# Two row tiles of a state-space stage moved ahead in a fused state-space and MLP kernel

## The chip, the cores and the metric

The kernel runs on one NeuronCore of a Trainium2 chip. The metric is the device time of one execution in microseconds (us); less is better. Five engines work side by side, each in the order of its own instruction stream: TensorE (PE), VectorE (DVE), ScalarE (ACT), GpSimd (POOL) and SyncE (SP), which here issues nearly all loads and stores. PSUM, into which PE writes, has eight banks of 512 float32 columns.

## The reference, cut to what matters

The input x has 2048 rows of 640. Two branches are computed and mixed, row by row, by a gate:

```python
g = sigmoid((x * gate_w).sum(-1, keepdims=True))
# branch a: a diagonal complex state-space layer
Lam_bar = exp(dt * Lam);  Bu = x @ B_bar.T          # P = 640 complex states
h[t] = Lam_bar * h[t-1] + Bu[t]                     # t = 0 .. 2047
a = 2 * real(hseq @ Cmat.T) + x * Dskip
# branch b: an MLP
b = gelu(x @ w1 + b1) @ w2 + b2                     # 640 -> 1728 -> 640
return g * a + (1 - g) * b
```

## The kernel before, in words

Time is cut into four chunks of 512 rows (CH). A chunk passes through four stages.

`ssm(c)` is the state stage. For each of five row tiles of 128 states (ks), PE multiplies x by the real and the imaginary part of B (BT_re, BT_im; five matmuls of 512 columns each), ACT copies both results out of PSUM to bf16 (`bu`, L602), and VectorE runs `scan_ops`: three products (f1 to f3) with tables of cosines and sines (TCOS, TSIN), which turn the complex recurrence into two real ones, two scans with the factor r_c (f4, L548), and three products back (f6 to f8) into `hs`. ACT turns the scan's end for the next chunk (`carry`, four small instructions, L556).

`ff1(c)` is the first MLP layer: thirteen tiles of 128 hidden columns (kf = 0 to 12), each of five matmuls of 512 columns (L300), and a gelu on ACT into `gel` (L309). W1 lies in three strips, w1a (tiles 0 to 5), w1b (6 to 9) and w1c (10 to 13). The last tile (`last_tile`, L324) is computed the other way round, on a bank that ACT first fills with its bias (`last_bank`, L317). Its last column is the gate: gate_w is copied into w1c as one more column (L441, POOL). ACT writes the tile's gelu to `gelN` and SP turns it with two transposing DMAs (L332).

`fin_b(c)` is the second MLP layer as a Strassen product: seven half-size products (L697) from sums of blocks of gel and W2. Three weight sums, TA, TB and TC, are built once, while chunk 1's `ff1` runs: ACT writes the negated W2 blocks to TA and TB (`w_minus`, L647), POOL adds the others with accumulating DMAs (`w_plus`, L642). `fin_a(c)` multiplies the states by C (L775), and VectorE mixes both branches with the gate columns `gcol` (L613 to L615, from `gates`), L780. `fold(ks)` multiplies the factor (Lam_bar - 1) / Lam into C, ACT first (L504, L506) and VectorE then (L510); it needs nothing of the scan. The last chunk's C product is a Strassen product too (`fin_s`, L837).

The order of work is written out by hand and is the program order of each engine. VectorE's order is set by a planner: `Clock` holds estimated times of PE, ACT and DVE; `later` queues a VectorE step with a due time and a cost, `let_out` issues those that by their estimated start come before a given time, `dve_now` first lets out what is due and then issues its own step. `small` holds the carries for ACT until PE's clock has passed their due time (`settle`). The estimates change only the order, not the work.

SP's order around the change: w1a strips 4 and 3 (L132), w1b (L164), w1c (L166), b1x (L182), four transposing loads of B (L184, L185: BT_re and BT_im of row tiles 0 and 1, then of 2 to 4), the transposing load of x's second chunk (L186), and, behind chunk 0's last tile, the gelN transposes (L332), W2 (`load_w2`, L197 to L206) and C (L209, L210).

Of the kernel before, what the change touches and what calls it, by code (L numbers as in the profile page):

```python
# [10 lines left out]
ALU = mybir.AluOpType  # L11
# [31 lines left out]
def kernel(  # L43
# [32 lines left out]
    def bank(dtype=F32):  # L76
        return ps.tile([P, CH * 4 // (4 if dtype == F32 else 2)], dtype, name="bank")
# [53 lines left out]
    def load_w1a(queue, kd):  # L131
        queue.dma_start(out=w1a[kd], in_=B_w1[kd * P:(kd + 1) * P, 0:cut1])  # L132
# [27 lines left out]
    load_turned(H)  # L160
    load_w1a(nc.sync, 4)
    load_w1a(nc.sync, 3)
    for kd in range(KD):
        nc.sync.dma_start(out=w1b[kd], in_=B_w1[kd * P:(kd + 1) * P, cut1:cut2])  # L164
    for t, k0, k1 in ((w1c_lo, 0, 3), (w1c_hi, 3, KD)):
# [14 lines left out]
    for i, m in enumerate((1.0, float(CH), float(CH // 2), float(2 * HC - 2))):  # L180
        nc.gpsimd.memset(tf[:, i:i + 1], m)
    nc.sync.dma_start(out=b1x[:, 0:F_LAST], in_=B_b1[F - F_LAST:F].rearrange("(o d) -> o d", o=1).to_broadcast([P, F_LAST]))  # L182
    for r0, r1, part in ((0, KSA * P, 0), (KSA * P, KS * P, 1)):
        nc.sync.dma_start_transpose(out=BT_re[part][:], in_=A_B_re[r0:r1, :])  # L184
        nc.sync.dma_start_transpose(out=BT_im[part][:], in_=A_B_im[r0:r1, :])  # L185
    nc.sync.dma_start_transpose(out=xT[1][:], in_=x2d[CH:2 * CH, :])  # L186
    nc.gpsimd.memset(gelN[:, :, F_LAST:P], 0.0)
    for k in range(2):
# [19 lines left out]
    def load_CT():  # L208
        nc.sync.dma_start_transpose(out=CT_re[:], in_=A_C_re[:, :])  # L209
        nc.sync.dma_start_transpose(out=CT_im[:], in_=A_C_im[:, :])  # L210
# [7 lines left out]


    class Clock:  # L220
        pe = 3.4
        act = 12.0
        dve = 0.0

# [204 lines left out]
        ff1_mm(banks[kf], 0, kf, 3, 0, CH, False, 3)  # L429
    for kf in range(FA):  # L430
        ff1_act(banks[kf], 0, kf)
    two_banks = [bank(), bank()]
    for kd in range(KD):
        for i in range(2):
            ff1_mm(two_banks[i], 0, FA + i, kd)
    for i in range(2):
        ff1_act(two_banks[i], 0, FA + i)
    nc.scalar.activation(out=thr[:], in_=dtl[:], func=ACT.Tanh, scale=0.5)
    act(0.2)
    for t, k0, k1 in ((w1c_lo, 0, 3), (w1c_hi, 3, KD)):  # L440
        nc.gpsimd.tensor_copy(out=t[:, :, n1c - 1:n1c], in_=colB[:, k0:k1].rearrange("p (k o) -> p k o", o=1))  # L441
    ff1(0, FA + 2)
    load_w2()
    load_CT()

    for dst, r in ((sq, 0), (cq, 1)):
        nc.vector.tensor_copy(out=dst[:].rearrange("p (n k) -> p k n", n=NQ), in_=FSC[:, r * KS:(r + 1) * KS, 0:NQ])
# [9 lines left out]

    nsL = col("nsL")
    nc.gpsimd.tensor_scalar(out=nsL[:], in0=sL, scalar1=-1.0, scalar2=None, op0=ALU.mult)
    nc.gpsimd.tensor_scalar(out=inv[:, KS:2 * KS], in0=thr[:], scalar1=-1.0, scalar2=1.0, op0=ALU.mult, op1=ALU.add)  # L460
    nc.gpsimd.tensor_scalar(out=thr[:], in0=thr[:], scalar1=1.0, scalar2=None, op0=ALU.add)
    around(TCOS, cM, sM, ALU.subtract, ALU.add)
    around(TSIN, sM, cM, ALU.add, ALU.subtract)
    nc.vector.tensor_copy(out=TCOS[:, :, HB:HB + HC], in_=FC)
# [6 lines left out]
    nc.vector.tensor_scalar(out=TSIN[:, :, HB - 1:0:-1], in0=TSIN[:, :, HB + 1:CH], scalar1=-1.0, scalar2=None, op0=ALU.mult)  # L471
    nc.vector.tensor_copy(out=TSIN2[:, :, 0, CH - 1:0:-1], in_=TSIN[:, :, 1:CH])
    nc.vector.reciprocal(out=inv[:], in_=inv[:])
    ck.dve = 20.0


    c2re = col("c2re"); n2re = col("n2re"); n2im = col("n2im")

    def factors():
        tt = lambda o, a, b, op: nc.gpsimd.tensor_tensor(out=o, in0=a, in1=b, op=op)  # L480
        a_c = col("a_c"); b_c = col("b_c")
        den = inv[:, 0:KS]
        tt(r_c[:], thr[:], inv[:, KS:2 * KS], ALU.mult)
        tt(a_c[:], r_c[:], cth, ALU.mult)
        tt(b_c[:], r_c[:], sth, ALU.mult)
        nc.gpsimd.tensor_scalar(out=a_c[:], in0=a_c[:], scalar1=-1.0, scalar2=None, op0=ALU.add)
        nc.gpsimd.tensor_scalar(out=den, in0=den, scalar1=2.0, scalar2=None, op0=ALU.mult)
        tt(q1[:], a_c[:], lre_c, ALU.mult)
        tt(q2[:], b_c[:], lim_c, ALU.mult)
        tt(q1[:], q1[:], q2[:], ALU.add)  # L490
        tt(c2re[:], q1[:], den, ALU.mult)
        tt(q1[:], a_c[:], lim_c, ALU.mult)
        tt(q2[:], b_c[:], lre_c, ALU.mult)
        tt(q1[:], q1[:], q2[:], ALU.subtract)
        tt(n2im[:], q1[:], den, ALU.mult)
        nc.gpsimd.tensor_scalar(out=n2re[:], in0=c2re[:], scalar1=-1.0, scalar2=None, op0=ALU.mult)
# [26 lines left out]
    def scan_ops(c, ks, bu, ready):  # L523
        wide = lambda t: t[:, ks:ks + 1, :].to_broadcast([P, 2, CH])
        sines = TSIN2[:, ks, :, :]
        s = {}

        def tt(o, a, b, op):
            nc.vector.tensor_tensor(out=o, in0=a, in1=b, op=op)  # L529

        def f1():
            s["mc"] = work.tile([P, 2, CH], BF16, name="wa", bufs=1)
            tt(s["mc"][:], wide(TCOS), bu[:], ALU.mult)

        def f2():
            s["ms"] = work.tile([P, 2, CH], BF16, name="wb", bufs=1)
            tt(s["ms"][:], sines, bu[:], ALU.mult)

        def f3():
            s["v"] = work.tile([P, 2, CH], BF16, name="v", bufs=1)  # L540
            tt(s["v"][:], s["mc"][:], s["ms"][:, ::-1, :], ALU.add)

        def f4(ri):
            if ri == 0:
                settle(1)
                s["g"] = work.tile([P, 2, CH], BF16, name="g")
            init = 0.0 if c == 0 else carry[:, ri, ks:ks + 1]
            nc.vector.tensor_tensor_scan(s["g"][:, ri, :], r_c[:, ks:ks + 1].to_broadcast([P, CH]),  # L548
                                         s["v"][:, ri, :], init, ALU.mult, ALU.add)

        def f5():
            g = s["g"]

            def turn_carry():
                m = work.tile([P, 2], F32, name="e1")
                one = lambda out, i, sc, b: nc.scalar.activation(out=out, in_=g[:, i, CH - 1:CH], func=ACT.Identity,  # L556
                                                                 scale=sc[:, ks:ks + 1], bias=b)
                one(m[:, 0:1], 1, nsL, 0.0)
                one(m[:, 1:2], 0, sL, 0.0)
                one(carry[:, 0, ks:ks + 1], 0, cL, m[:, 0:1])  # L560
                one(carry[:, 1, ks:ks + 1], 1, cL, m[:, 1:2])
                ck.act += 0.6

            small.append((ck.dve + 2.0, turn_carry))

        def f6():
            s["no"] = work.tile([P, 2, CH], BF16, name="wa", bufs=1)
            tt(s["no"][:], wide(TCOS), s["g"][:], ALU.mult)

        def f7():  # L570
            s["ns"] = work.tile([P, 2, CH], BF16, name="wb", bufs=1)
            tt(s["ns"][:], sines, s["g"][:], ALU.mult)

        def f8():
            to = lambda t: t.rearrange("p r (i t) -> p r i t", i=2)
            dst = hs[c][:].rearrange("p i r k t -> p r i k t")[:, :, :, ks, :]
            tt(dst, to(s["no"][:]), to(s["ns"][:, ::-1, :]), ALU.subtract)

        later(ready, 0.68, f1)
        later(0, 0.62, f2)  # L580
        later(0, 0.65, f3)
        later(0, 1.27, lambda: f4(0))
        later(0, 1.21, lambda: f4(1))
        if c < NCH - 1:
            later(0, 0.0, f5)
        later(0, 0.69, f6)
        later(0, 0.62, f7)
        later(0, 0.64, f8, c)

    def ssm(c, at={}):  # L590
        hs[c] = hsp.tile([P, 2, 2, KS, HT], BF16, name="hs")
        for ks in range(KS):
            if ks in at:
                at[ks]()
            bu = work.tile([P, 2, CH], BF16, name="bu", bufs=8)
            for ri, BT in enumerate((BT_re, BT_im)):
                p = bank()
                for kd in range(KD):
                    nc.tensor.matmul(p[:], lhsT=BT[ks >= KSA][:, kd, (ks % KSA if ks < KSA else ks - KSA) * P:][:, 0:P], rhs=xT[c][:, kd, :],  # L599
                                     start=(kd == 0), stop=(kd == KD - 1))  # L600
                    pe(CH)
                nc.scalar.activation(out=bu[:, ri, :], in_=p[:], func=ACT.Identity)  # L602
                act(0.6)
            scan_ops(c, ks, bu, ck.act)
            let_out(ck.pe)
            settle()


    def gates(c):
        sl = slice(c * TPC, (c + 1) * TPC)  # L610

        def f():
            nc.vector.tensor_scalar(out=gcol[:, 0, sl], in0=gz[:, sl], scalar1=0.5, scalar2=0.5, op0=ALU.mult, op1=ALU.add)  # L613
            nc.vector.tensor_scalar(out=gcol[:, 1, sl], in0=gz[:, sl], scalar1=-0.5, scalar2=0.5, op0=ALU.mult, op1=ALU.add)
            nc.vector.tensor_scalar(out=gcol[:, 2, sl], in0=gz[:, sl], scalar1=0.5, scalar2=-0.5, op0=ALU.mult, op1=ALU.add)  # L615

        dve_now(ck.pe, 0.2, f)


    HALVES = ((0, HD), (HD, D))  # L620
# [280 lines left out]
    def sums(c):  # L901
        return {0: lambda: minus_c(c), 1: lambda: minus_d(c)}

    ssm(0)
    gel_tile(1)

    ff1(1, 0, {3: lambda: (w_minus(0), w_plus(TA, B12)),
               5: lambda: (w_minus(1), w_plus(B12, TB)),
               9: lambda: (first_sums(), w_plus(TB, TA), w_plus(TC, TB))})
    gates(0)  # L910
    ssm(1, {3: lambda: fold(0)})
# [63 lines left out]
```

## Time and profile before

| | |
|---|---|
| median of three runs | 208.58 us (208.19 to 208.94) |
| the profiled execution | 208.8 us, of which the profile's span is 207.0 us |
| granted PE clock | 1.00 |
| PE busy | 201.8 us (98%) |
| VectorE busy | 180.5 us (87%) |
| ACT busy | 143.9 us (69%) |
| chunk 0: `ff1`, then `ssm` on PE | first w1a matmul 3.96, w1b 11.44, w1c 16.03, last tile 19.27, `ssm` 19.88 us |
| chunk 1: `ff1`, last tile, `ssm` on PE | 30.67, 45.37, 45.97 us |
| first state product on VectorE | 22.87 us |

Times on the profile's axis count from the start of the span. A row of the list of waits names the instruction that waited, then what released it, then the total, the count and the longest. A row of the chain has start, length and what it was; "x20" counts merged instructions. SPq is the sequencer of SP, which issues DMAs; its rows in a timeline last as long as the issue, and the data lands later. PEld is PE's weight load, which runs ahead of the matmuls.

### The profile page before, as it was taken

The numbers are of one execution on the slowest core, as the hardware profiler recorded it, in microseconds if no ns is written. First come the engines' busy times: TensorE is split into PE (matmuls) and PEld (weight loads), VectorE is DVE, ScalarE is ACT, GpSimd is POOL, SyncE is SP. The second block draws the span as 40 slices with busy tenths as digits, with TensorE's granted clock in tenths as the row PEclk, the third lists the DMA queues.
The fourth block names the chain that finished last, engine by engine and source line by source line (L and its number), as shares of the span: only waits on it lengthen the run. The fifth ranks groups of instructions, "written<-read, shape, count | busy, mean of one in ns | idle before, by whom it ended". The sixth has DMA issues, their size and how long they took to land.

```text
span 207.0 us, 3588 instructions
## 1 busy us (share of the span) xinstructions
PE 201.8 (98%) x1311; PEld 120.3 (58%) x1311; DVE 180.5 (87%) x282; ACT 143.9 (69%) x291; POOL 45.6 (22%) x81
## 2 busy tenths in 40 slices
PE   8999999999999999999999999999999999999993
PEld 5745444444467644675457777544447777777762
DVE  2694599999499999699999999999999999998673
ACT  4699656999888799992666893358986595067720
POOL 8426100313410410031001061200420136016000
PEclk9999999999999999999999999999999999999999
DMA  6999989999899070269913279920675729949703
GB/s 190 233 206 213 177 220 298 176 212 218 152 181 220 16 117 6 69 115 245 205 42 66 59 139 216 258 85 0 79 158 105 161 79 194 194 130 164 124 2 127
DMA packets 45126, 30.28 MB, mean 146 GB/s; under 512 B 26834, under 2 KB 42548, under 8 KB 45108
## 3 DMA queue, kind: packets, MB, share of 16 engines
q0 software_dynamic: 6448, 12.53, 35.3%
q1 hardware_dynamic: 38084, 17.03, 34.6%
q10 hardware_dynamic: 576, 0.49, 0.8%
q8 instruction: 10, 0.16, 0.3%
q14 instruction: 8, 0.07, 0.1%
HBM read 7.79 MB, written 2.62 MB: 50 GB/s over the span
## 4 chain that ended last, share of the span: by engine, by line
PE 76%; SPq 14%; ACT 4%; DMA 3%; issue 1%; DVE 0%; DVEq 0%; ACTq 0%
PE bank L697 26%; PE bank L775 16%; PE bank L599 16%; PE bank L300 14%; PE bank L837 4%; DMA w_sb<-in_B_w_dram 3%; SPq L184 2%; SPq L185 2%; SPq L186 2%; ACT gel L309 2%; SPq L197 1%; SPq L157 1%; SPq L332 1%; SPq L164 1%; PE bank L324 1%
## 5 line engine op out<-in xcount | busy, mean ns | idle before, releaser
L548 DVE TENSOR_TENSOR_SCAN g<-r_c,carry,v 128x512 bf16<-128x512 f32 x30 | 37.5, 1274 | 0.9
L602 ACT ACTIVATE bu<-bank 128x512 bf16<-128x512 f32 x40 | 23.5, 596 | 21.0 <-PE bank L599 21.0
L309 ACT ACTIVATE gel<-bank,colB 128x512 bf16<-128x512 f32 (+1 forms) x52 | 33.0, 692 | 3.9 <-PE bank L300 3.5
L697 PEld LDWEIGHTS <-gel 128*128 128x128 bf16 x280 | 27.3, 98 | 11.1 <-issue 0.2
L775 PEld LDWEIGHTS <-hs 128*128 128x128 bf16 x240 | 23.4, 98 | 9.0
L697 PE MATMUL bank<-w_sb,gel 128*128 128x320 bf16 x168 | 24.3, 299 | 0.0
L300 PEld LDWEIGHTS <-w1a_sb 128*128 128x128 bf16 x162 | 13.9, 97 | 12.2 <-issue 0.3
L775 PE MATMUL bank<-CT_re,hs 128*128 128x320 bf16 x120 | 20.2, 299 | 0.0
L775 PE MATMUL bank<-CT_im,hs 128*128 128x320 bf16 x120 | 20.2, 299 | 0.0
L717 ACT ACTIVATE gb<-bank,gcol 128x320 f32<-128x320 f32 x32 | 15.8, 524 | 5.2 <-PE bank L697 5.2
L529 DVE TENSOR_TENSOR wa<-TCOS,bu 128x1024 bf16<-128x1024 bf16 x20 | 13.8, 690 | 5.8 <-ACT bu L602 5.1
L709 ACT ACTIVATE bank<-bank 128x320 f32<-128x320 f32 x16 | 6.8, 423 | 14.3 <-DVE ot L780 8.1
L599 PEld LDWEIGHTS <-BT_im 128*128 128x128 bf16 x100 | 9.8, 98 | 11.8
L599 PEld LDWEIGHTS <-BT_re 128*128 128x128 bf16 x100 | 9.6, 98 | 11.0
L529 DVE TENSOR_TENSOR hs<-wa,wb 128x1024 bf16<-128x1024 bf16 x20 | 13.8, 690 | 0.6
L529 DVE TENSOR_TENSOR v<-wa,wb 128x1024 bf16<-128x1024 bf16 x20 | 13.8, 690 | 0.6
L300 PE MATMUL bank<-xA,w1a_sb 128*128 128x128 bf16 (+2 forms) x102 | 14.1, 291 | 0.2 <-DVE xA L269 0.2
L529 DVE TENSOR_TENSOR wa<-TCOS,g 128x1024 bf16<-128x1024 bf16 x20 | 13.8, 689 | 0.4
L529 DVE TENSOR_TENSOR wb<-TSIN,g 128x1024 bf16<-128x1024 bf16 x20 | 13.7, 684 | 0.0
L529 DVE TENSOR_TENSOR wb<-TSIN,bu 128x1024 bf16<-128x1024 bf16 x20 | 13.7, 684 | 0.0
L300 PEld LDWEIGHTS <-w1b_sb 128*128 128x128 bf16 x80 | 7.8, 98 | 9.8 <-DMA w1b_sb<-in_B_w_dram 0.8
L697 PEld LDWEIGHTS <-N 128*128 128x128 bf16 x112 | 11.0, 98 | 4.3
(183 smaller groups left out, 370.2 us busy)
## 6 DMA issues: line engine op xcount, KB each, us to landing
out_dram<-ot SPq DMA_DIRECT2D x15, 160.0 KB, 4.6
w_sb<-in_B_w_dram SPq DMA_DIRECT2D x4, 480.0 KB, 6.5
gb<-gq POOLq DMA_DIRECT2D x6, 320.0 KB, 5.9
gel<-N POOLq DMA_DIRECT2D x4, 448.0 KB, 4.6
xn<-in_A_x_dram SPq DMA_DIRECT2D x10, 160.0 KB, 3.6
N<-gel POOLq DMA_DIRECT2D x3, 448.0 KB, 4.4
gel<-gel POOLq DMA_DIRECT2D x3, 448.0 KB, 6.8
N<-N POOLq DMA_DIRECT2D x3, 448.0 KB, 7.7
```

Of the source, the lines that this page charges most:

```text
L184: nc.sync.dma_start_transpose(out=BT_re[part][:], in_=A_B_re[r0:r1, :])
L300: nc.tensor.matmul(p[:, t0:t1], lhsT=w, rhs=xT[c][:, kd, t0:t1], start=(kd == 0) if first is None else first, stop=(kd == last), skip_grou ...
L309: nc.scalar.activation(out=dst, in_=src, func=ACT.Gelu_apprx_tanh, bias=b1_c[p0:p1, kf:kf + 1])
L529: nc.vector.tensor_tensor(out=o, in0=a, in1=b, op=op)
L548: nc.vector.tensor_tensor_scan(s["g"][:, ri, :], r_c[:, ks:ks + 1].to_broadcast([P, CH]), s["v"][:, ri, :], init, ALU.mult, ALU.add)
L599: nc.tensor.matmul(p[:], lhsT=BT[ks >= KSA][:, kd, (ks % KSA if ks < KSA else ks - KSA) * P:][:, 0:P], rhs=xT[c][:, kd, :], start=(kd == 0 ...
L602: nc.scalar.activation(out=bu[:, ri, :], in_=p[:], func=ACT.Identity)
L697: nc.tensor.matmul(p[:, 0:HD], lhsT=lhs[:, s, j * P:(j + 1) * P], rhs=rhs[:, s, :], start=fresh and s == 0, stop=s == KH - 1, skip_group_c ...
L709: nc.scalar.activation(out=quad[j][dst][:, 0:HD], in_=quad[j][src][:, 0:HD], func=ACT.Identity)
L717: nc.scalar.activation(out=gbs[ti][:, h * HD:(h + 1) * HD], in_=quad[j][name][:, 0:HD], func=ACT.Identity, scale=gcol[:, 1, ti:ti + 1])
L775: nc.tensor.matmul(p[:, 0:d1 - d0], lhsT=hs[c][:, a // H, j // KS, j % KS, (a % H) * P:][:, 0:P], rhs=CT[:, j % KS, d0:d1], start=False, s ...
L837: nc.tensor.matmul(t[j][:, d0:d1], lhsT=A[i][:, k, j * P:(j + 1) * P], rhs=B[i][:, k, d0:d1], start=fresh and k == 0, stop=k == KS - 1, sk ...
```

## The change

The transposing loads of BT_re and BT_im for row tiles 0 and 1 are issued by SP right behind w1a, ahead of w1b, w1c and b1x. The matmuls and evictions of row tiles 0 and 1 of chunk 0's state stage (`inputs(0, range(KSA))`) are issued right behind the six w1a tiles: first both BT_re groups, then both BT_im groups. The rest of chunk 0's `ff1`, `load_w2` and `load_CT` follow, and `ssm(0)` is left with row tiles 2 to 4.

On POOL, the two instructions that prepare `inv` and `thr` and the product r_c come ahead of the copy of the gate columns into w1c. In chunk 1's `ff1`, the two negations of W2 with their accumulating DMAs move from tiles 3 and 5 to tiles 5 and 7. The planner's PE clock starts at 5.9 instead of 3.4, VectorE's is 17.8 instead of 20.0 behind the tables, three of its costs are larger, and `gates` is due by ACT's clock in chunks 1 to 3. With these clocks the planner issues the folds and the gate columns later in VectorE's order.

```diff
     load_w1a(nc.sync, 4)
     load_w1a(nc.sync, 3)
+    def load_BT(part, r0, r1):
+        nc.sync.dma_start_transpose(out=BT_re[part][:], in_=A_B_re[r0:r1, :])
+        nc.sync.dma_start_transpose(out=BT_im[part][:], in_=A_B_im[r0:r1, :])
+    load_BT(0, 0, KSA * P)
     for kd in range(KD):
         nc.sync.dma_start(out=w1b[kd], in_=B_w1[kd * P:(kd + 1) * P, cut1:cut2])
...
-    for r0, r1, part in ((0, KSA * P, 0), (KSA * P, KS * P, 1)):
-        nc.sync.dma_start_transpose(out=BT_re[part][:], in_=A_B_re[r0:r1, :])
-        nc.sync.dma_start_transpose(out=BT_im[part][:], in_=A_B_im[r0:r1, :])
+    load_BT(1, KSA * P, KS * P)
...
-        pe = 3.4
+        pe = 5.9
...
     for kf in range(FA):
         ff1_act(banks[kf], 0, kf)
-    two_banks = [bank(), bank()]
-    ...
     nc.scalar.activation(out=thr[:], in_=dtl[:], func=ACT.Tanh, scale=0.5)
     act(0.2)
-    for t, k0, k1 in ((w1c_lo, 0, 3), (w1c_hi, 3, KD)):
-        nc.gpsimd.tensor_copy(out=t[:, :, n1c - 1:n1c], in_=colB[:, k0:k1]...)
-    ff1(0, FA + 2)
-    load_w2()
-    load_CT()
+    nc.gpsimd.tensor_scalar(out=inv[:, KS:2 * KS], in0=thr[:], ...)
+    nc.gpsimd.tensor_scalar(out=thr[:], in0=thr[:], ...)
...
     nc.vector.reciprocal(out=inv[:], in_=inv[:])
-    ck.dve = 20.0
+    nc.gpsimd.tensor_tensor(out=r_c[:], in0=thr[:], in1=inv[:, KS:2 * KS], op=ALU.mult)
+    for t, k0, k1 in ((w1c_lo, 0, 3), (w1c_hi, 3, KD)):
+        nc.gpsimd.tensor_copy(out=t[:, :, n1c - 1:n1c], in_=colB[:, k0:k1]...)
+    ck.dve = 17.8
+
+    def inputs(c, rows):
+        bus = [work.tile([P, 2, CH], BF16, name="bu", bufs=8) for _ in rows]
+        ready = []
+        for ri, BT in enumerate((BT_re, BT_im)):
+            for bu, ks in zip(bus, rows):
+                p = bank()
+                for kd in range(KD):
+                    nc.tensor.matmul(p[:], lhsT=BT[ks >= KSA][:, kd, ...][:, 0:P], rhs=xT[c][:, kd, :], ...)
+                    pe(CH)
+                nc.scalar.activation(out=bu[:, ri, :], in_=p[:], func=ACT.Identity)
+                ready.append(act(0.6))
+        return list(zip(bus, ready[-len(bus):]))
+
+    early = inputs(0, range(KSA))
+    two_banks = [bank(), bank()]
+    ...                                  # w1b tiles 6 and 7, as before
+    ff1(0, FA + 2)
+    load_w2()
+    load_CT()
...
-        later(0, 0.62, f2)
-        later(0, 0.65, f3)
+        later(0, 0.65, f2)
+        later(0, 0.75, f3)
...
-        later(0, 0.64, f8, c)
+        later(0, 0.7, f8, c)
...
-            scan_ops(c, ks, bu, ck.act)
+            scan_ops(c, ks, *(given[ks] if ks < len(given) else inputs(c, [ks])[0]))
...
-        dve_now(ck.pe, 0.2, f)                                       # in gates(c)
+        dve_now(ck.act + 0.3 if c > 0 else ck.pe, 0.2, f)
...
-    ssm(0)
+    ssm(0, {}, early)
     gel_tile(1)
-    ff1(1, 0, {3: lambda: (w_minus(0), w_plus(TA, B12)),
-               5: lambda: (w_minus(1), w_plus(B12, TB)),
+    ff1(1, 0, {5: lambda: (w_minus(0), w_plus(TA, B12)),
+               7: lambda: (w_minus(1), w_plus(B12, TB)),
                9: lambda: (first_sums(), w_plus(TB, TA), w_plus(TC, TB))})
```

More of the change, by code (lines that the diff above doesn't have):

```diff
@@ L431 @@
         ff1_act(banks[kf], 0, kf)
-    two_banks = [bank(), bank()]
[L433 to L437, printed above, removed]
     nc.scalar.activation(out=thr[:], in_=dtl[:], func=ACT.Tanh, scale=0.5)
     act(0.2)
-    for t, k0, k1 in ((w1c_lo, 0, 3), (w1c_hi, 3, KD)):
-        nc.gpsimd.tensor_copy(out=t[:, :, n1c - 1:n1c], in_=colB[:, k0:k1].rearrange("p (k o) -> p k o", o=1))
-    ff1(0, FA + 2)
-    load_w2()
-    load_CT()
+    nc.gpsimd.tensor_scalar(out=inv[:, KS:2 * KS], in0=thr[:], scalar1=-1.0, scalar2=1.0, op0=ALU.mult, op1=ALU.add)
+    nc.gpsimd.tensor_scalar(out=thr[:], in0=thr[:], scalar1=1.0, scalar2=None, op0=ALU.add)
     for dst, r in ((sq, 0), (cq, 1)):
@@ L459 @@
     nc.gpsimd.tensor_scalar(out=nsL[:], in0=sL, scalar1=-1.0, scalar2=None, op0=ALU.mult)
-    nc.gpsimd.tensor_scalar(out=inv[:, KS:2 * KS], in0=thr[:], scalar1=-1.0, scalar2=1.0, op0=ALU.mult, op1=ALU.add)
-    nc.gpsimd.tensor_scalar(out=thr[:], in0=thr[:], scalar1=1.0, scalar2=None, op0=ALU.add)
     around(TCOS, cM, sM, ALU.subtract, ALU.add)
@@ L473 @@
     nc.vector.reciprocal(out=inv[:], in_=inv[:])
-    ck.dve = 20.0
+    nc.gpsimd.tensor_tensor(out=r_c[:], in0=thr[:], in1=inv[:, KS:2 * KS], op=ALU.mult)
+    for t, k0, k1 in ((w1c_lo, 0, 3), (w1c_hi, 3, KD)):
+        nc.gpsimd.tensor_copy(out=t[:, :, n1c - 1:n1c], in_=colB[:, k0:k1].rearrange("p (k o) -> p k o", o=1))
+    ck.dve = 17.8
[6 more added lines that the diff above has]
+                for kd in range(KD):
+                    nc.tensor.matmul(p[:], lhsT=BT[ks >= KSA][:, kd, (ks % KSA if ks < KSA else ks - KSA) * P:][:, 0:P], rhs=xT[c][:, kd, :],
+                                     start=(kd == 0), stop=(kd == KD - 1))
+                    pe(CH)
[4 more added lines that the diff above has]
+    two_banks = [bank(), bank()]
+    for kd in range(KD):
+        for i in range(2):
+            ff1_mm(two_banks[i], 0, FA + i, kd)
+    for i in range(2):
+        ff1_act(two_banks[i], 0, FA + i)
+    ff1(0, FA + 2)
+    load_w2()
+    load_CT()
     c2re = col("c2re"); n2re = col("n2re"); n2im = col("n2im")
@@ L482, in factors @@
         den = inv[:, 0:KS]
-        tt(r_c[:], thr[:], inv[:, KS:2 * KS], ALU.mult)
         tt(a_c[:], r_c[:], cth, ALU.mult)
@@ L587, in scan_ops, with ssm @@
         later(0, 0.62, f7)
-        later(0, 0.64, f8, c)
-    def ssm(c, at={}):
+        later(0, 0.7, f8, c)
+    def ssm(c, at={}, given=()):
         hs[c] = hsp.tile([P, 2, 2, KS, HT], BF16, name="hs")
@@ L594, in ssm @@
                 at[ks]()
[L595 to L603, printed above, removed]
-            scan_ops(c, ks, bu, ck.act)
+            scan_ops(c, ks, *(given[ks] if ks < len(given) else inputs(c, [ks])[0]))
             let_out(ck.pe)
```

## The prediction

> **What bounds the kernel now.** I read the page's busy table first, then the list of who waited for whom, then the chain of work in order of time between 28 and 57 us, then the timelines of SP, ACT and DVE over the first 50 us.
>
> ```profile
> span 207.0 us, 3588 instructions
> PE 201.8 (98%) x1311; PEld 120.3 (58%) x1311; DVE 180.5 (87%) x282; ACT 143.9 (69%) x291; POOL 45.6 (22%) x81
> ```
>
> TensorE (PE) is the bound. Its rows run at an unchanging pace: a group of five 512-column matmuls starts every 1.08 us (L599 starts at 19.88, 20.96, 22.04), a whole state stage takes 10.79 us each time, a fin_b 13.31 us, a fin_a 10.87 us. The change adds and removes no matmul, so it can only move the places in which PE stands still. The list of waits has few of them:
>
> ```profile
> PEld L300 <- DMA w1b_sb<-in_B_w_dram: 0.8, 2, 0.6
> PE bank L324 <- ACT bank L317: 0.5, 1, 0.5
> DVE wa L529 <- ACT bu L602: 5.1, 1, 5.1
> DVE CT_re L510 <- issue: 3.1, 1, 3.1
> ```
>
> The first row is W1's second strip arriving late. Weight loads run ahead of matmuls, so the 0.8 us costs PE less: the 20 w1b matmuls of chunk 0 start at 11.44 and the next kind at 16.03, 4.59 us for work of 4 x 1.08 = 4.32 us, a loss of 0.27 us. The second row is at 45.4 us. The chunk-1 FF1 starts at 30.67 and its 13 tiles need 14.03 us (the same stage takes 14.03 at 70.44), so the last tile could start at 44.70; it starts at 45.37, a loss of 0.67 us. Together 0.94 us: that is all that PE can win here. The other two rows are VectorE's own idle time, 5.05 us before the first scan and 3.13 us before the first fold; no PE wait of the list hangs on VectorE behind the front. So the five microseconds that the change gives VectorE shorten nothing by themselves.
>
> Where the 0.67 us comes from is in the chain:
>
> ```profile
> 28.99 0.03 SPq L338
> 29.02 0.03 issue
> 29.05 1.40 SPq L338
> 30.45 0.04 issue
> 30.49 6.06 DMA w_sb<-in_B_w_dram
> 36.55 0.02 issue
> 36.58 0.02 ACTq L647
> 36.59 0.04 issue
> 36.64 0.57 ACT TA L647
> 37.21 1.41 issue
> 38.62 1.25 ACT gel L309 x2
> 39.86 1.96 ACT TB L647
> 41.82 1.73 ACT gel L309 x3
> ```
>
> ScalarE's first negation of W2 (TA) waits until 36.64 for W2's last rows to land, and everything behind it on ScalarE is late, down to the bias bank of the last tile (L317, done at 45.32), for which PE waits. SP issues W2 only behind the two transposes of gelN (L332, issued at 23.46); those need gelN, which ScalarE wrote by 20.87 + 0.38 = 21.25, so before the change SP was late (its xB transpose ended at 23.34), not gelN.
>
> **The change part by part.**
>
> *Twenty matmuls brought forward on PE.* Tiles 0 and 1 of the state stage take 20 x 0.216 = 4.32 us and stand right behind the first strips, at 11.44. What follows of chunk 0's FF1 shifts by 4.32; the stage behind it is shorter by as much. Without waits chunk 1's FF1 starts at 30.67 - 0.27 = 30.40. PE now needs BT_re at 11.44, BT_im at 13.60, w1b from 15.76 (its fifth strip at 17.5), w1c at 20.08.
>
> *Two transposes moved up on SP, past w1b, w1c and b1x.* SP is free at 6.39, where the first w1b is issued now. The four BT transposes took 3.20, 1.68, 1.62 and 2.65 us of SP and landed 4.3 to 5.4 us after their issue. So BT_re lands between 6.39 + 4.3 = 10.7 and 11.8; BT_im is issued between 8.0 and 9.6 and lands between 12.3 and 15.0. PE waits between 0 and 0.4 us for the one, 0 and 1.4 for the other. The five w1b follow at 9.7 to 12.3, each 0.47 us after the last, landing 3.3 to 5.1 us after issue: the fifth between 14.9 and 19.3, against 17.5. I call the whole front wait w: at least 0, at most 1.8 us. I take w = 0.2, by the row nearest to that place: the xA transposes just ahead took 1.28 us for 6 blocks, and the queue at 6.39 holds two short strips, so the issue should be near the low end; BT_re then arrives about when it is needed and w1b in time. The 0.27 us of today's w1b wait goes. Front: -0.27 + w.
>
> Of the Trainium skill, "DMA: Bandwidth & Descriptors", section "Queues, rings and completion order", speaks against this move: a DMA engine consumes the descriptors of a ring in order, so w1b's data cannot pass the transposes. The trace agrees in so far as the moved transposes' second (issued 13.53, nothing ahead) landed in 4.3 us and the first (10.29, behind w1c) in 5.0. The same page, section "Latency and other measured facts", gives 261 GB/s for transposes; by it, as an estimate, one 327,680-byte transpose is 1.3 us of data, both would be through before w1b's hour, and w would be 0.
>
> *ScalarE's four evictions of the early tiles.* They stand behind the six gelus (11.37 + 6 x 0.59 = 14.9) and the tanh; at about 0.55 us each they end at 17.2, when PE has just finished their banks (15.76). The next gelu has its bank at 17.7. Nothing is delayed. If w moved PE, these move with it.
>
> *POOL and DVE.* inv, thr and r_c stand ahead of the gate columns of w1c, which waited 3.99 us for a DMA (14.96); they now come behind, and need be there only for the last tile at 23.3. VectorE's tables end at 17.81 (reciprocal) as today; r_c follows by 18.2, the first scan needs it at 20. So the first state product starts at 17.9 instead of 22.87, 5.0 us sooner, for no PE time.
>
> *The last tile of chunk 0, gelN and W2.* This is the bill. Behind the moved matmuls, gelN ends at 21.25 + 4.32 - 0.27 + w = 25.3 + w. SP, done with the same list at about 23.4 as today, now waits for it 1.9 us, and the gelN transposes, the four W2 loads and the rest start 25.3 - 23.46 = 1.84 us + w later. They can't catch up: between 30 and 35 us the DMA engines are full (share 1.17, 304 GB/s), and that stream is W2. So W2's last rows land at 36.55 + 1.84 + w = 38.4 + w.
>
> *The negations two tiles later.* TA now stands behind gelu 4 instead of gelu 2, TB behind gelu 6 instead of gelu 4. Gelu 4 ends at 30.40 + 5.39 + 0.2 + 0.7 = 36.7 + w. So ScalarE still stands still for 1.7 us (1.43 today), with TA at 38.4 + w. Behind it, by the planner's clocks: TA 1.98, gelus 5 and 6 2 x 0.57, the carry of tile 2 0.93 (its scan, 5 us earlier now, is long done), TB 1.96, gelus 7 and 8 1.14, bias bank 0.40: 7.55 in all, against 45.32 - 36.64 = 8.68 today, since two gelus stand ahead now. The bank is there at 45.95 + w; PE could start the last tile at 30.40 + 14.03 = 44.43 + w, so it waits 1.5 us instead of 0.67.
>
> *Sum.* The last tile of chunk 1 starts at 46.0 + w instead of 45.37: +0.63 + w = +0.8 us. Behind it the order of ScalarE's evictions against PE is as today, and PE has no other idle time worth 0.2 us, so the end moves with it. The POOL chain behind TA and TB (the accumulating DMAs to TC) starts 1.8 to 2.7 us later; its last issue at 56.23 landed some 4.8 us later, 61.0, and TC is read at 66.4, so 2.7 us are covered; without that cover they would cost what exceeds 5.4. The other planner edits (costs of 0.65, 0.75, 0.7, gates by ScalarE's clock, PE's clock at 5.9) only reorder VectorE: the first fold comes behind the first product of chunk 1, so its 3.13 us idle go, and the first output of chunk 0's fin_a comes behind some 1.9 us of scan work; eight banks cover that, so I put it at nothing, with -0.2 to +0.5 as bounds (PE's own smallest idle, and the one bank wait seen).
>
> The profiled execution took 208.8 us around its span of 207.0; the median of the runs is 208.58. Span 207.8, profiled 209.6, median 209.4.
>
> **The rivals.**
>
> *Faster: the bias bank is in time.* If W2 lands by 36.8 + w, whether because SP's wait costs W2 less than 1.84 us (its stream finding the engines free of the xB transpose) or because ScalarE is further on, both idle times go: -0.94 + 0.2 = -0.7, 207.8 us. It decides at the start of TA: every 0.1 us earlier than 38.4 is 0.1 us won, and 0.6 us earlier is no change. Against it: 1.6 us would have to be found in a stream that is full.
>
> *Much slower: PE starves at 11 to 18 us.* If the transposes issue at 3.2 us each and BT_im and w1b land at the late ends, w is 1.8 us; with more queueing than any row shows, 3. Everything behind shifts: +0.63 + 1.8 to 3 = 2.4 to 3.6 us, 211 to 212.2 us. For it: the one transpose issued into a full queue took 3.20 us. Against it: the queue at 6.39 is shorter.
> "TensorE: Matmul & The Clock Gate", section "Part 1: The HAM clock gate (the \"warmup\" mystery)", has PE fall to half its clock after about 3.4 us of idling; the granted clock here is 1.00 throughout, with no idle time over 0.8 us. By the page the cost would rise above w only past 3.4 us, which I don't count.
>
> *It does nothing:* front wait and W2's delay balance the 0.94 us, 208.6.
>
> **How the numbers follow.** Forecast 0.55, its own range 208.9 to 210.2; faster 0.24; starved 0.12; nothing 0.09. A measurement here can tell about 0.3%, 0.63 us, from no change. The forecast's 0.8 us stands close to that bound: of its 0.55 I give 0.40 to slower, 0.13 to same, 0.02 to faster; the faster rival gives 0.22 to faster and 0.02 to same; starved all to slower; nothing all to same. That makes 0.24, 0.24, 0.52. The range goes from 207.7 (0.94 us less) to 211.2 (w at its bound with the W2 delay).
>
> **What would show it.** Right: TA starts on ScalarE near 38.5, released by a W2 DMA; PE waits 1.3 to 1.8 us for L317 near 46; the first state product on VectorE near 17.9; gelN transposes issued near 25.3; PE idle at 11.4 under 0.5 us. Wrong: no PE wait for L317 (the faster rival), a PE wait for BT_im or w1b over 1 us (starved), or a new PE wait for VectorE behind 85 us, which no row of before suggests.

## The result, and the profile after

The changed kernel takes 210.44 us, the median of four runs (210.26 to 210.74), against 208.38 us for the kernel before in the same comparison (208.04 to 208.94). The ratio is 1.0097, 95% interval 1.007 to 1.0125: slower by 2.06 us, beyond the 0.3% that can be told apart. The forecast was 209.4 us, slower, with a range up to 211.2: the direction and the chain of waits came true, the size was more than twice the forecast. The profiled execution of after took 210.74 us around its span of 209.0. Below, medians are over all executions of a kernel, and ratios leave out those that took over 1.5% longer than the fastest of their kernel (two of e1's twelve, three of e9's twelve, five of e10's nine); of these only one of e10's was profiled, so why e1 and e9 have them isn't shown.

The page and the list of waits of after:

```profile
span 209.0 us, 3595 instructions
PE 203.0 (97%) x1311; PEld 121.7 (58%) x1311; DVE 181.1 (87%) x282; ACT 144.2 (69%) x291; POOL 52.5 (25%) x81
```
```profile
PE bank L328 <- ACT bank L321: 1.6, 1, 1.6
ACT TA L657 <- DMA w_sb<-in_B_w_dram: 1.9, 1, 1.9
```

Line numbers have moved: L328 is the last tile (L324 before), L321 the bias bank (L317), L657 the negations (L647), L336 the gelN transposes (L332), L201 the large W2 loads (L197), L479 the B products (L599). The same wait for the bias bank that cost PE 0.5 us now costs 1.6. PE waits neither for B's data nor for w1b, and VectorE's 5.1 and 3.1 us rows are gone, as forecast. Part of what VectorE gained in front comes back at the end as idle time: it waits 4.2 us at 189.1 us for ScalarE (`gb`, L832), 0.8 us at the same place before. The total of POOL rose from 45.6 to 52.5 us.

The timelines of ScalarE and of SP (start, length, line, operation) show who lets whom go:

```profile
26.02 0.38 ACT L331 ACTIVATE gelN<-bank 128x256 bf16<-128x256 f32 x1
```
```profile
19.22 3.73 SPq L190 DMA_TRANSPOSE xB<-in_A_x_dram  x1
26.49 2.46 SPq L336 DMA_TRANSPOSE gel<-gelN  x2
28.99 2.92 SPq L201 DMA_DIRECT2D w_sb<-in_B_w_dram  x4
```

SP is through with xB at 22.95 and issues nothing until gelN is written at 26.40: 3.5 us of standing still, and W2 stands behind it. From there the chain in order of time runs to PE's wait:

```profile
33.47 6.19 DMA w_sb<-in_B_w_dram
...
39.74 2.07 ACT TA L657
41.81 1.15 ACT gel L313 x2
42.96 0.36 ACT e L575 x2
43.33 0.08 ACT carry L575
43.40 0.10 issue
43.50 0.38 ACT carry L575
43.88 1.96 ACT TB L657
45.84 1.15 ACT gel L313 x2
46.99 0.29 ACT bank L321
47.27 0.04 issue
47.32 0.77 PE bank L328 x20
```

Chunk 1's FF1 begins at 31.51 and has 14.03 us of work, so its last tile could start at 45.54; it starts at 47.32, a loss of 1.78 us.

Followed further back, the profile's chain leaves SP for a false cause: it comes to the second gelN transpose through small POOL instructions (`q L500`). Before as after, the two transposes take 2.46 us together with 0.04 us between them, so nothing waited for POOL there. A chain names an inferred releaser at every step; whether the engine stood idle before that step is the test of it.

### The profile page after: what moved, and what is told of

Read it like the earlier page. It is cut to its first block, busy times and chain, and to the rows that moved or that the text cites. A ratio compares the mean times of both kernels' runs of the same rounds, so it can differ in the third digit from the quotient of the medians.

```text
span 209.0 us, 3595 instructions
## 1 busy us (share of the span) xinstructions
PE 203.0 (97%) x1311; PEld 121.7 (58%) x1311; DVE 181.1 (87%) x282; ACT 144.2 (69%) x291; POOL 52.5 (25%) x81
## 4 chain that ended last, share of the span: by engine, by line
PE 79%; DVE 5%; POOL 4%; ACT 4%; DMA 3%; SPq 3%; issue 1%; DVEq 0%; ACTq 0%; POOLq 0%
PE bank L707 26%; PE bank L785 16%; PE bank L479 15%; PE bank L304 15%; PE bank L847 4%; DMA w_sb<-in_B_w_dram 3%; POOL q L500 2%; SPq L201 1%; PE bank L263 1%; ACT gel L313 1%; ACT TA L657 1%; PE bank L328 1%; ACT TB L657 1%; SPq L342 1%; SPq L336 1%
## 5 line engine op out<-in xcount | busy, mean ns | idle before, releaser
L313 ACT ACTIVATE gel<-bank,colB 128x512 bf16<-128x512 f32 (+1 forms) x52 | 33.5, 686 | 6.8 <-PE bank L304 6.5
L304 PEld LDWEIGHTS <-w1a_sb 128*128 128x128 bf16 x162 | 15.0, 104 | 12.0
L719 ACT ACTIVATE bank<-bank 128x320 f32<-128x320 f32 x16 | 6.8, 423 | 15.0 <-PE bank L707 14.9
L790 DVE SCALAR_TENSOR_TENSOR ot<-bank,gcol,gb 128x320 bf16<-128x320 f32 x24 | 12.7, 542 | 4.6 <-PE bank L785 3.2
L479 PEld LDWEIGHTS <-BT_im 128*128 128x128 bf16 x100 | 9.8, 98 | 11.8
L479 PEld LDWEIGHTS <-BT_re 128*128 128x128 bf16 x100 | 9.6, 98 | 11.0
L304 PE MATMUL bank<-xA,w1a_sb 128*128 128x128 bf16 (+2 forms) x102 | 15.1, 309 | 0.0
```

What stands on the lines that cost most here:

```text
L304: nc.tensor.matmul(p[:, t0:t1], lhsT=w, rhs=xT[c][:, kd, t0:t1], start=(kd == 0) if first is None else first, stop=(kd == last), skip_grou ...
L313: nc.scalar.activation(out=dst, in_=src, func=ACT.Gelu_apprx_tanh, bias=b1_c[p0:p1, kf:kf + 1])
L719: nc.scalar.activation(out=quad[j][dst][:, 0:HD], in_=quad[j][src][:, 0:HD], func=ACT.Identity)
L790: nc.vector.scalar_tensor_tensor(out=ot[:, d0:d1], in0=p[:, 0:d1 - d0], scalar=gcol[:, 0, ti:ti + 1], in1=gbs[ti][:, d0:d1], op0=ALU.mult, ...
```

## The experiments

The theories: the chain gelN, SP, W2, TA, bias bank makes the loss (theory A); PE's waits at the front, for BT and w1b, make it (theory B); the planner's new order of VectorE makes part of it (theory C); and, once before's profile was in question, the 0.94 us of PE idle time in it only covers a front that varies, and isn't something that a kernel regularly has to win (theory D).

**e1: after, with W2's loads ahead of the gelN transposes on SP.** Nothing else moves on any engine.

```diff
-    ff1(0, FA + 2)
-    load_w2()
+    load_w2()          # without load_e(0) and TC
+    ff1(0, FA + 2)
+    load_TC()          # load_e(0), then TC
     load_CT()
```

> The changed kernel, but W2's loads stand on SP ahead of chunk 0's last tile, so that they don't wait for gelN; the load of the gelu's last rows and TC's stay behind it. Theory A (the loss is W2's late start, passed on by ScalarE to the bias bank of chunk 1's last tile): TA starts right behind gelu 4, near 37.5 us, PE waits for the bias bank under 0.2 us instead of 1.6, and the time is 210.4 - 1.6 = 208.8 us. Theory B (the loss is PE waiting at the front for the moved transposes and w1b): nothing changes behind it, 210.2 to 210.5 us. Theory C (the new order on VectorE costs PE time behind 50 us): also 210.2 to 210.5 us.

Measured: 208.76 us, 1.68 us less than after; against before the ratio is 1.0016 (0.9997 to 1.0034). ScalarE's timeline of e1:

```profile
37.07 2.06 ACT L660 ACTIVATE TA<-w_sb 128x2240 bf16<-128x2240 bf16 x1
44.19 0.40 ACT L323 ACTIVATE bank<-b1x 128x260 f32<-128x260 bf16 x1
```

TA no longer waits, ScalarE starts on the bias bank at 44.19 instead of 46.88, and PE has no wait behind its front. The chain is thus shown as the cause of 1.68 of the 2.06 us; that e1 differs from before at all is not shown, as its interval holds 1. POOL is as slow in e1 as in after (52.5 us), so it had no part.

**e2: after, with only the bias bank's ACT instruction ahead of TA.** W2 stays late.

```diff
     ...                                  # in ff1: for chunk 1, tile 5 instead of tile 9
+            if kf == (5 if c == 1 else KF - 5 if c > 0 else KF - 3):
+                last = last_bank(c)
             if kf in at:
                 at[kf]()
-            if kf == (KF - 5 if c > 0 else KF - 3):
-                last = last_bank(c)
```

> The changed kernel, but ScalarE fills the bias bank of chunk 1's last tile ahead of the first negation (TA) instead of behind gelu 8; W2 stays as late as it is. Theory A: PE no longer waits at the last tile, 1.6 us less, 208.8 us, if no other bank is late; if ScalarE's backlog reaches the next bank that PE needs, part of the 1.6 us comes back as a wait at the start of chunk 1's state stage, 209.2 to 209.8 us. Theories B and C: 210.2 to 210.5 us.

Measured: 209.16 us, ratio 1.0034 (1.0022 to 1.0045). The wait for L321 is gone; a shorter one appears some 13 us later, at the start of fin_b, where PE adds to a bank into which ScalarE must first copy another product (`fork`, L719):

```profile
PE bank L707 <- ACT bank L719: 1.0, 1, 1.0
```

So ScalarE's backlog, not this one bank, is what PE meets: taking the bank out of the queue saves 1.28 us by the medians, less than e1's 1.68, and part of the wait comes back at the next place where PE needs ScalarE. (The profiled execution, 209.83 us, is the longest of its twelve.)

**e3: before, with the negations at tiles 5 and 7** as in the change: `{3: ..., 5: ...}` becomes `{5: ..., 7: ...}`, and no more.

> The kernel before, with only the two negations of W2 two tiles later (tiles 5 and 7 instead of 3 and 5). Theory A: W2 lands at 36.6 us as before, TA stands behind gelu 4 and hardly waits, the bias bank is done near 44.5 instead of 45.3, and PE's idle 0.67 us at the last tile goes: 207.8 us, 0.6 less than before. Rival (the later negations make the accumulating DMAs to TC late): 208.4 us or more, with a PE wait for TA, TB or TC near 63 to 67 us.

Measured: 208.44 us, ratio 0.9997 (0.9983 to 1.0012). A miss: 0.6 us less was expected, and the interval leaves no room for it. In its profile the gelN transposes are issued at 22.24, not 23.46, TA starts at 37.15 without a wait, and PE has no idle time behind the front. There was next to nothing to win, which put the profile of before itself in question.

**e5 and e6: before and after again, unchanged,** one execution each.

> The kernel before, unchanged, profiled once more, to see how firm its 0.94 us of PE idle time are. In its first profile PE finished the first strips of W1 at 11.44 us, earlier than in any other profile here (11.8 to 12.6). Theory D (that idle time is cover for a front that is usually later, so the change could never have won it): with strips ending near 12.0 the w1b wait and the wait at chunk 1's last tile together are under 0.4 us, and the span is still 206.4 to 207.0 us. The prediction's reading (the idle time is there in every execution): 0.8 to 1.1 us of it, whatever the front.

> The changed kernel, profiled once more. Theory A: PE waits 1.4 to 2.0 us for the bias bank at chunk 1's last tile whatever the front does, since the whole chain from gelN to W2 to the first negation starts on PE and moves with it; the span is 195.2 us behind the end of the first strips (in the first profile 12.55 us), plus that wait, to within 0.3 us, plus what PE waits for BT. Rival (the wait is a matter of the late front of the first profile): with strips ending near 12.0 the wait is under 1 us.

Measured: before 208.03 us (span 206.2), after 210.52 us (span 208.7). SP's timeline in the first profile of before:

```profile
19.62 3.72 SPq L186 DMA_TRANSPOSE xB<-in_A_x_dram  x1
23.46 2.46 SPq L332 DMA_TRANSPOSE gel<-gelN  x2
25.96 2.97 SPq L197 DMA_DIRECT2D w_sb<-in_B_w_dram  x4
```

Page, SP's and ScalarE's timeline of the second one:

```profile
span 206.2 us, 3577 instructions
```
```profile
19.06 2.90 SPq L186 DMA_TRANSPOSE xB<-in_A_x_dram  x1
22.09 2.46 SPq L332 DMA_TRANSPOSE gel<-gelN  x2
24.59 2.91 SPq L197 DMA_DIRECT2D w_sb<-in_B_w_dram  x4
```
```profile
34.99 2.06 ACT L647 ACTIVATE TA<-w_sb 128x2240 bf16<-128x2240 bf16 x1
43.26 0.41 ACT L317 ACTIVATE bank<-b1x 128x260 f32<-128x260 bf16 x1
```

W2's first issue is at 24.59 instead of 25.96, TA at 34.99 without a wait, and PE stands nowhere behind its front. Both idle times of the first profile are absent. After repeats its loss; from the list of waits of PE and its weight loads in e6:

```profile
PE bank L328 <- ACT bank L321: 1.7, 1, 1.7
PEld L479 <- DMA BT_re<-in_A_B_re_dram: 0.5, 1, 0.5
```

The profiles obey one sum. Let F be the time at which PE is through with the w1a strips. The next group starts at F, in before and in after:

```profile
11.44 4.75 PE L300 MATMUL bank<-xA,w1b_sb 128*128 128x512 bf16 x20
```
```profile
12.55 2.32 PE L479 MATMUL bank<-xA,BT_re 128*128 128x512 bf16 x10
```

In e6 it starts at 12.27, as it waits 0.19 us for BT_re; F is 12.08 there.

| profile | F | span | span - F | PE idle behind F |
|---|---|---|---|---|
| before | 11.44 | 207.0 | 195.56 | 0.27 + 0.67 |
| before again (e5) | 11.59 | 206.2 | 194.61 | none |
| e3 | 12.01 | 206.6 | 194.59 | none |
| after | 12.55 | 209.0 | 196.45 | 1.78 |
| after again (e6) | 12.08 | 208.7 | 196.62 | 0.19 + 1.82 |
| e1 | 11.93 | 206.5 | 194.57 | none |
| e2 | 12.45 | 208.0 | 195.55 | 0.98 |

Span = F + 194.6 + PE's idle time; e4 and e7 (with its 1.08 us of added matmuls) fit it to 0.1 us, and e8's span is 0.2 us longer than the sum. The first profile of before had the earliest front and lost more than that again. The other profile of before and that of e3 have no idle time to be won; how often an execution of before has it, two profiles can't tell, but e3's interval and e7 say that it is little in the median.

**e7: before, with five more 512-column matmuls (1.08 us) behind the w1a strips,** their results unused. If there is idle time to swallow it, less than 1.08 us comes through.

```diff
+    for _ in range(5):
+        nc.tensor.matmul(pT[:, 0:CH], lhsT=ones(P), rhs=ones(CH), start=True, stop=True, ...)
```

> The kernel before with five more 512-column matmuls on PE (1.08 us, results unused) behind the first strips of W1. Theory D (little cover is left in a usual execution): 0.7 to 1.1 us longer, 209.1 to 209.5 us. The prediction's reading (0.94 us of idle time that a PE delay could fill): 0.1 to 0.3 us longer, 208.5 to 208.7 us.

Measured: 209.12 us against 208.38, ratio 1.0036 (1.0023 to 1.005): 0.74 us, between 0.5 and 1.0 by the interval. So the usual cover is some 1.08 - 0.74 = 0.3 us, and less than 0.94 by the whole interval. In its own profile (F 12.44, span 208.2) all of the 1.08 us came through.

**e4: after, with one early row tile instead of two:** `early = inputs(0, range(1))`.

> The changed kernel with one row tile ahead instead of two; the DMA order is the same. Theory A: gelN comes 2.2 us earlier, W2 starts close to where it did before the change, and the wait at the bias bank falls from 1.6 to about 0.3 us at most: 209.0 us. Theory B (PE waits at the front for BT_re): the wait for BT_re stays as it is and w1b is wanted 2.2 us earlier, so 210.4 us or more. Theory C: 210.2 to 210.5 us.

Measured: 209.2 us, ratio 1.0037 (1.0022 to 1.0052). The time is near theory A's 209.0, but for another reason in part. TA at 37.96 doesn't wait, and no wait for the bias bank is left; but with only one tile's BT_re products to bridge, PE waits for BT_im:

```profile
PE bank L479 <- DMA BT_im<-in_A_B_im_dram: 0.8, 1, 0.8
```

The second early tile thus gives BT_im its time (after has no such wait), and pays for it in gelN's delay.

**e8: after, with the old planner constants:** PE's clock from 3.4, VectorE's 20.0, costs 0.62, 0.65, 0.64, `gates` due by PE's clock.

> The changed kernel with the planner as before the change (PE's clock from 3.4, VectorE's 20.0 behind the tables, the old costs, gates due by PE's clock). Theory A: the planner's order is no part of the loss, as long as the carries stay behind the bias bank or ahead of the negation: 210.0 to 210.7 us. Theory C (VectorE's new order costs PE): 209.5 us or less.

Measured: 209.75 us (209.34 to 211.49), ratio 1.0085 (1.0052 to 1.0118): between the two expectations, and 0.69 us less than after by the medians. This interval and that of after (1.007 to 1.0125) overlap, so the times alone don't show a difference. The profile does; the wait in its list and ScalarE's timeline:

```profile
PE bank L328 <- ACT bank L321: 0.7, 1, 0.7
```
```profile
39.41 2.07 ACT L657 ACTIVATE TA<-w_sb 128x2240 bf16<-128x2240 bf16 x1 [1.47 <-DMA w_sb<-in_B_w_dram]
41.39 1.25 ACT L313 ACTIVATE gel<-bank,colB 128x512 bf16<-128x512 f32 x2
42.53 2.07 ACT L657 ACTIVATE TB<-w_sb 128x2240 bf16<-128x2240 bf16 x1
44.49 1.26 ACT L313 ACTIVATE gel<-bank,colB 128x512 bf16<-128x512 f32 x2
45.63 0.41 ACT L321 ACTIVATE bank<-b1x 128x260 f32<-128x260 bf16 x1
```

TA is as late as in after, but the four small instructions of a carry (42.96 to 43.88 in the chain of after, 0.92 us) no longer stand between TA and TB. PE loses 0.82 us at the last tile (46.08 against 45.26) instead of 1.78. In these profiles, one of e8 and two of after, the planner thus has a part of some 0.96 us, and it works through ScalarE's queue ahead of the bias bank, not through PE waiting for VectorE as theory C had it.

**e9: e1, with the two row tiles behind W1's tiles 6 and 7 instead of ahead of them,** and BT's transposes behind w1b on SP.

```diff
-    load_BT(0, 0, KSA * P)               # ahead of w1b on SP
     ... w1b loads
+    load_BT(0, 0, KSA * P)
-    early = inputs(0, range(KSA))        # ahead of W1's tiles 6 and 7
     ... W1's tiles 6 and 7
+    early = inputs(0, range(KSA))
```

> The changed kernel with W2's loads ahead of gelN's, as in e1_w2_early, and besides with the two row tiles and their two transposes one step later: on PE behind W1's tiles 6 and 7, on SP behind the five loads of w1b. If what was left of the loss in e1_w2_early (208.76 against 208.42 us) is PE waiting for BT in executions with an early front, it goes: 208.2 to 208.5 us, and the profile shows no PE wait for BT_re, BT_im or w1b over 0.3 us. If it is something else behind the front, it stays: 208.7 to 208.9 us.

Measured: 209.6 us, 208.52 to 221.21, ratio 1.0044 (1.0017 to 1.0072). A miss. The profiled execution (208.84 us) has no PE idle time behind F and fits the sum: 12.42 + 194.58 = 207.0. The median lies higher because five of its twelve executions take 210 us and more; why, no profile shows.

**e10: before, with e1's edit.**

> The kernel before with W2's loads ahead of gelN's on SP and nothing else. In a usual execution W2 is in time already, so theory D expects 208.1 to 208.4 us, at most 0.3 us less, with no PE wait for the bias bank of chunk 1's last tile. The prediction's reading (0.67 us of that wait in every execution): 207.7 us.

Measured: 212.25 us (208.91 to 216.2), ratio 1.0099 (1.006 to 1.0137). A miss, and its profile (215.9 us, among the longest of its nine executions; span 214.1) shows a wait that no other profile here has. The waits, then SP's timeline:

```profile
ACT xA L507 <- DMA CT_im<-in_A_C_im_dram: 6.6, 1, 6.6
PE bank L700 <- ACT bank L712: 5.8, 1, 5.8
```
```profile
37.67 6.52 SPq L211 DMA_TRANSPOSE CT_re<-in_A_C_re_dram  x1
44.24 11.12 SPq L212 DMA_TRANSPOSE CT_im<-in_A_C_im_dram  x1
```

The transposing load of CT_im holds SP for 11.12 us (7.22 in before, 5.65 in e5); ScalarE waits for it with the first fold, and PE for ScalarE, whose copy for fin_b (`fork`, L712) stands behind that fold. In the same stretch POOL's first accumulating DMAs for TA, issued at 37.93, let the next one go at 52.48; in e5 they were issued at 37.35 and the next at 43.92, with the second held for them until 47.48. Here the accumulating DMAs begin 0.26 us behind CT_re; in e5 they begin 2.15 us behind it. That they hinder each other is argued from this overlap and was not isolated. With W2 early in the kernel of before, there is nothing to save (as in e5), and the long transposes are new.

No version beat before. By the sum, a kernel with no PE idle time behind F is at its floor of F + 194.6, and before is there in one of its two profiles.

## Why the prediction was right, and where it was not

*PE as the bound, VectorE's five microseconds worth nothing:* right. The first state product started at 18.83 on VectorE (17.9 forecast; the front was 1.1 us later), 4 us sooner than before, and no PE time came of it.

*The front, w = 0.2:* right in size. PE waited 0 us for BT_re in after and 0.19 in e6, and the w1b wait went: w1b landed from 14.11 to 15.57, behind BT_im (13.73) as issued, and was wanted from 16.87. One reading under it was wrong. The 5.0 us to landing belong to the transpose issued at 15.25; for the one issued at 10.29 the trace has no landing, and the one issued at 13.53 had it ahead in the queue. BT_im then took 5.7 us in after, beyond the 5.4 allowed. The starved rival (1.8 to 3 us) was not seen; 0.8 us in e4 is its nearest trace.

*gelN, SP, W2:* right step by step. Forecast from F: gelN 13.86 us behind it, measured 13.85; from the transposes' issue to TA 13.1, measured 13.25; from TA to the end of the bias bank 7.55, measured 7.54; PE ready for the last tile 32.99 us behind F, measured 32.99. The loss at the last tile was put at 1.5 us and is 1.8. The faster rival, in which the bias bank is in time, is refuted by PE's wait in both profiles of after, and "it does nothing" by the interval. That 210.44 us lies inside the range is in part luck: the upper end was drawn for the starved front, which did not come (and 208.58 + 0.63 + 1.8 is 211.0, not 211.2).

*The step that failed* is the credit, "Together 0.94 us: that is all that PE can win here", and with it the sum +0.63 + w. The 1.5 us were set against 0.67 us of the same wait and 0.27 us of w1b's wait that before has in its profiled execution. e5 and e3 have neither, and e7 finds room for some 0.3 us in the usual execution. The first profile of before differs from the others twice over: its front was the earliest of all (11.44), and its SP was 1.4 us later with gelN than in e5 (23.46 against 22.09). Counted from F, W2's first load is issued at 14.52 us in it, at 13.00 in e5 and at 16.44 in after. So the change delays W2 by 1.92 us against the first, about the 1.84 forecast, but by 3.44 us against e5. Without the credit the forecast's own steps give 1.5 + 0.2 = 1.7 us; PE's idle times in the two profiles of after are 1.78 and 2.01, against 2.06 measured in the times.

*The planner edits at nothing (-0.2 to +0.5):* mis-sized by the profiles. The carry of 0.93 us was in the forecast's 7.55, but not charged to the planner, whose order puts it there; without these edits PE's idle time in e8 is 0.96 us shorter and the median 0.69 us lower, the latter not clear of noise. In e1, where ScalarE has time, the same carry costs nothing.

*Left open:* e1 has no PE wait and still lies 0.34 us above before by the medians, which is not clear of noise. The fronts of after's kind in these profiles run from 11.84 to 12.55, those of before's from 11.44 to 12.44; whether the change makes the front later by some tenths, too few profiles tell.

## What to carry to other kernels

Idle time that one profile shows on the engine that bounds the kernel is no credit until a second profile shows it too: take two, line up their fronts, and subtract. When work on the bound engine is brought forward, list what its displaced neighbours release; here the matmuls that moved cost nothing, but the tile pushed back released a load on another queue later, and that load's reader stood in front of the bank that the bound engine needed. The cure is at the queue (e1: independent loads ahead of a dependent one), and it too has to be looked at for what it now meets (e10).

## What the runs showed of the hardware that was not expected

**PE's pace in the first microseconds differs between executions.** The same nine 128-column matmuls, in PE's timeline of before and then of after:

```profile
4.23 0.67 PE L300 MATMUL bank<-xA,w1a_sb 128*128 128x128 bf16 x9
```
```profile
4.65 1.17 PE L304 MATMUL bank<-xA,w1a_sb 128*128 128x128 bf16 x9
```

That is 74 ns against 130 ns each, and the faster pace begins at about 3.4 us in before, 6.7 in after, 4.2 in e6 and 4.6 in e5. The granted clock reads 1.00 in both stretches, so only the pace shows it. It is a good part of why F varies; PE's waits of 0.7 to 0.8 us for rows of x, in e2 and e7, are another.
The Trainium skill, "TensorE: Matmul & The Clock Gate", section "Part 1: The HAM clock gate (the "warmup" mystery)", has PE start at half clock and speed up at the end of a window of about 3.4 us that runs free of the kernel's start. That the moment varies agrees with it. The page has it vary by 0.5 us to either side; here it lies anywhere between 3.4 and 6.7 us, and the measurement decides. No run here isolates the cause.

**A PE idle time of 5.8 us costs more than itself.** Windows of e10 (stretch, length, busy time and count of PE, its weight loads, VectorE, ScalarE, POOL, then granted clock, DMA share, GB/s):

```profile
56.00:60.00 4.00, 2.62 (x18) 1.57 (x17) 0.00 (x0) 0.33 (x1) 0.85 (x1) 1.00 1.11 171
60.00:64.00 4.00, 0.00 (x0) 0.00 (x0) 2.64 (x7) 4.00 (x11) 1.70 (x2) 0.59 1.05 152
64.00:68.00 4.00, 3.56 (x16) 2.10 (x16) 3.93 (x5) 2.70 (x6) 0.86 (x1) 0.56 1.19 241
68.00:72.00 4.00, 4.00 (x31) 2.90 (x30) 3.64 (x6) 2.77 (x5) 0.86 (x1) 1.00 1.11 256
```

The clock falls to 0.59 and 0.56 and is back by 68: in the window at 64, PE does 16 matmuls where the next does 31. The 14 matmuls behind the wait, in PE's timeline of e10, take 67.83 - 64.44 = 3.39 us, while the same number takes 1.91 us right after them, so the slow clock costs some 1.5 us on top of the wait, in this one execution:

```profile
64.44 3.55 PE L700 MATMUL bank<-w_sb,gel 128*128 128x320 bf16 x14 [5.82 <-ACT bank L712]
67.83 2.06 PE L700 MATMUL bank<-w_sb,N 128*128 128x320 bf16 x14
69.74 2.06 PE L700 MATMUL bank<-TB,N 128*128 128x320 bf16 x14
```

PE's wait of 1.62 us in after leaves the granted clock at 1.00.

**Small POOL instructions slow down beside VectorE's products.** One instruction on five columns, in POOL's timeline of before and of after:

```profile
18.55 0.23 POOL L486 TENSOR_SCALAR a_c<-a_c 128x5 f32<-128x5 f32 x1
```
```profile
20.96 1.18 POOL L505 TENSOR_SCALAR a_c<-a_c 128x5 f32<-128x5 f32 x1
```

The factors took 2.8 us before, between VectorE's tables and its first product (18.24 to 21.0), and 9.6 us after (20.20 to 29.8), with the products and scans running since 18.83. Nobody needs them before the first fold, near 55 us, so PE pays nothing; on a path to PE the sooner start of VectorE would have had a price.
The Trainium skill, "SBUF — State Buffer", section "SBUF: two separate sides", has VectorE and GpSimd share a pair of ports as a lock held for a whole instruction; an instruction of POOL that lasts as long as one of VectorE's (0.6 us for a product, some 1.2 for a scan) agrees with that. No run here isolates it.
